# A recurrent-memory transformer on one core: order of the first steps' loads, norms, value groups and output sums

## The chip, the core and the metric

The kernel runs on one core of a Trainium2 chip, as one launch. The metric is the device time of an execution in microseconds (us). Five engines work beside each other, each through its own list of instructions in order: TensorE (PE in the profile; its weight loads are PEld), VectorE (DVE), ScalarE (ACT), GpSimd (POOL) and SyncE (SP), which here issues loads and stores. ACT and POOL can issue loads as well. An engine waits at an instruction until the semaphores that it names are reached; what stands behind it waits too.

## The reference

Two layers of the same kind are applied one after the other, with the same weights. In each, attention over segments with a memory carried from segment to segment, and then a dense layer, each behind a layer norm and with a residual:

```
x = x + A(layernorm(x));  x = x + B(layernorm(x))      # layer 0
x = x + A(layernorm(x));  x = x + B(layernorm(x))      # layer 1

A:  mem = mem0                                          # 8 x 512
    for s in range(64):                                 # segments of 32 tokens
        h = concat([mem, xs])                           # 40 x 512
        q, k, v = h Wq, h Wk, h Wv                      # 32 heads of 128
        p = softmax(mask(q k^T / sqrt(128)))            # 40 x 40 for each head
        o = (p v) Wo                                    # 40 x 512
        mem = o[:8];  output o[8:]
B:  relu(x w1) w2                                       # 512 -> 1376 -> 512
```

x is 2048 x 512, all inputs are bfloat16. The memory makes the segments a chain: a step's queries and keys need the memory that the step before has made. The values of tokens do not depend on it and can be made at any time before.

## The kernel before

**Steps.** The work is written as 68 steps. Step k handles segment k of layer 0 and segment k - 4 of layer 1, where they exist (`layers`): steps 0 to 3 have layer 0 alone ("single"), steps 4 to 63 have both, steps 64 to 67 have layer 1 alone. Step 0 is written out in `first_step`, the others in `step`. In each: queries and keys of 16 heads (`qk`, tiles `qp`, copied by ACT to QT and by DVE to KT), the scores (`sp`), a softmax (`exponentials` and `softmax`: DVE `mx`, `es`, `sm`, ACT's exponential, the product P_sb or P1_sb), the same for the other 16 heads, turns of the probabilities (`tp`, PT0, PT_sb), their product with the values (`pv`), copies of that into OTm (memory rows) and OTx (token rows), and the output of the memory rows (`output_mem`, tile `wo`).

**The end of a step.** `new_memory` copies `wo` to `wm` on ACT, turns it on PE (`mt`), and copies `mt` twice: `to_values` into HTm, from which `memory_values` makes the memory's values (`vm`, copied by ACT to VmS), and `to_queries` into HT, from which the next step's `qk` starts. Some token rows travel with the memory rows ("ride") and are picked out by `output_ride` (`xp`). `prepare` makes the statistics for the next norm.

**Fillers.** Work that is not part of this chain is put in between. `output_x` makes the token rows of the step before from OTx, in parts named by `block`: where the rows are 32, either by quarters of the 512 columns (line 405: four matmuls of 128 columns for each head) or, where `by_heads` holds, by two heads and two halves at once (line 400: two matmuls of 256 columns for each head). `add_output` then sums the pieces into the residual R on DVE: by quarters four sums of 32x128 (line 470), by heads four sums of 32x256 (line 461). `dense_h` and `dense_y` make the dense layer of the step two before; `dense_y` is cut at `f_mid`, the rest comes after `output_mem` in the steps that are not `ahead` (1 and 2).

**Values.** `values0(p, n)` makes one group of layer 0's values: 64 tokens (pair p of segments) by 1024 columns (n and n + 1), eight matmuls into a bank `vp`, a copy by ACT to a staging tile, and a write to DRAM by SP (`vd`). The matmuls of a group can be parted (`lo`, `hi`). Pairs 1, 3, 5 and 7 have four groups each. Step 0 makes eleven of the twelve groups of pairs 1, 3, 5; `values_at` puts (5,6), (7,0) and (7,2) into step 1, (7,4) into step 2's `new_memory` and (7,6) into step 4. The values are read back into Vs by `load_values`. Staging tiles are slices of w1_sb and w2_sb in step 0 (`slots`, before the dense weights are loaded there), later tiles of the tag `vst` with five buffers, shared with VmS, `wm` and the input tiles 1 to 3.

**Inputs.** Input tile n holds tokens 128n to 128n + 127. It is loaded (`load_xb`), normed (`moments_x` on DVE with a power on POOL, `normalize` on DVE), and turned (`inputs_T`: four transposes on PE and a copy by ACT for the first four tiles) into xT0. `tokens_in` copies a segment's columns to HT on POOL.

**What sets the order.** PE, DVE, SP and POOL execute in the order in which the program is written (`manual_schedule`); ACT's order, and which buffer of a tag is taken, come from the planner. SP's list begins with the loads: input tile 0, half of Wq, mem0, input tile 1, half of Wk, half of Wv, then (`load_rest`) input tile 2, the other halves, Wo in five parts, input tile 3.

## Time and profile before

| what | value |
|---|---|
| time, median of 3 runs | 1578.87 us (1577.22 to 1578.91) |
| the profiled execution: its own time, its span | 1578.9 us, 1577.0 us |
| busy: PE, PEld | 1546.3 us (98%), 1283.1 us (81%) |
| busy: DVE, ACT, POOL | 1274.7 us (81%), 736.2 us (47%), 349.1 us (22%) |
| granted TensorE clock, mean | 1.000 |
| read from and written to HBM | 65.41 MB, 45.35 MB |

The span runs from the first to the last instruction; the execution's own time is 1.9 us longer. Busy is the time in which at least one instruction of the engine ran. In the page's 40 slices of the span (39.4 us each) PE is busy 0.5 of the first, 0.8 of the second and at least 0.9 of all that follow but the last, which has 0.8; the DMA engines are busy 0.9 of the first slice, 0.7 of the second and 0.1 to 0.4 after it. Step 0's first `qp` matmul starts at 16.34 us, step 1's at 51.83, step 2's at 72.62, step 3's at 93.08, step 4's at 111.99, step 5's at 135.25. After an instruction's line in the timeline, brackets give the idle time of its engine before it and what ended that.

### The profile page before, as it was taken

The page shows a single profiled execution, that of the slowest core. Times are in us where ns is not written, and L with a number is a line of the kernel's source. Part 1 is how long each engine was busy: PE and PEld are TensorE (multiplying, and loading weights), DVE is VectorE, ACT ScalarE, POOL GpSimd, SP SyncE. Part 2 cuts the span into 40 slices and gives each one's busy share as a digit, 9 for nine tenths or more (in the row PEclk, how much of TensorE's full clock was granted, in tenths as well). Part 3 has the DMA queues.
Part 4 walks back from the last instruction along what each step waited for, and adds up shares of the span by engine and source line. Part 5 has one row for each costly group of instructions (what it writes and reads, how often), then busy time and mean ns, then how long its engine had stood idle before and what let it go on. Part 6 is the DMA issues. An engine that isn't in the chain of part 4 may idle for free. (4 is left out here: it accounts for less than half of the span.)

```text
span 1577.0 us, 95035 instructions
## 1 busy us (share of the span) xinstructions
PE 1546.3 (98%) x42802; PEld 1283.1 (81%) x42802; DVE 1274.7 (81%) x3300; ACT 736.2 (47%) x1778; POOL 349.1 (22%) x670
## 2 busy tenths in 40 slices
PE   5899999999999999999999999999999999999998
PEld 3577888888888888889888888988888898888876
DVE  3578888888888888888888888888888888888866
ACT  3435445454544545454454545445454544545443
POOL 2012212222222222222122222212222221222110
PEclk9999999999999999999999999999999999999999
DMA  9733342444444344344433433343443333334331
GB/s 370 244 81 75 87 84 81 80 95 82 73 92 84 79 82 97 81 74 91 84 80 80 99 81 75 88 84 80 77 95 81 71 88 80 82 75 95 76 69 41
DMA packets 222133, 146.26 MB, mean 93 GB/s; under 512 B 123576, under 2 KB 216096, under 8 KB 221728
## 3 DMA queue, kind: packets, MB, share of 16 engines
q1 hardware_dynamic: 218560, 135.96, 37.5%
q8 instruction: 336, 5.51, 1.5%
q0 software_dynamic: 3072, 4.20, 1.1%
q14 instruction: 69, 0.57, 0.1%
q10 hardware_dynamic: 96, 0.03, 0.0%
HBM read 65.41 MB, written 45.35 MB: 70 GB/s over the span
## 5 line engine op out<-in xcount | busy, mean ns | idle before, releaser
L601 ACT CAST QT<-qp 128x480 bf16<-128x480 f32 (+3 forms) x408 | 201.1, 493 | 432.1 <-PE qp L595 432.0
L595 PE MATMUL qp<-HT,Wq_sb 128*128 128x80 bf16 (+1 forms) x8704 | 370.0, 200 | 1.8 <-POOL HT L828 1.2
L595 PEld LDWEIGHTS <-Wq_sb 128*128 128x128 bf16 x8704 | 325.2, 100 | 33.0 <-issue 25.9
L595 PE MATMUL qp<-HT,Wk_sb 128*128 128x80 bf16 (+1 forms) x8704 | 347.3, 200 | 1.5 <-DMA Wk_sb<-in_A_Wk_dram 1.2
L595 PEld LDWEIGHTS <-Wk_sb 128*128 128x128 bf16 x8704 | 319.5, 100 | 2.6 <-DMA Wk_sb<-in_A_Wk_dram 1.7
L668 POOL TENSOR_TENSOR P_sb<-es,sm 128x320 bf16<-128x320 f32 x185 | 130.6, 719 | 712.9 <-ACT QT L601 273.7
L603 DVE CAST KT<-qp 128x480 bf16<-128x480 f32 (+3 forms) x408 | 220.2, 565 | 35.4 <-PE qp L595 32.9
L647 DVE TENSOR_REDUCE mx<-sp 128x8 f32<-128x320 f32 x256 | 114.9, 486 | 133.3 <-PE sp L629 131.6
L377 PE MATMUL wox<-Wo_sb,OTx 128*64 128x256 bf16 x2880 | 174.1, 274 | 0.1
L377 PEld LDWEIGHTS <-OTx 128*64 128x64 bf16 x2880 | 150.0, 110 | 3.7 <-issue 0.6
L653 ACT ACTIVATE es<-es 128x320 f32<-128x320 f32 x256 | 109.5, 468 | 61.5 <-DVE es L651 61.0
L839 PE MATMUL vm<-Wv_sb,HTm 128*32 128x512 bf16 x2176 | 129.4, 379 | 1.8 <-DVE KT L603 1.0
L637 PE MATMUL wo<-Wo_sb,OTm 128*32 128x512 bf16 x2144 | 128.8, 380 | 0.5
L358 PE MATMUL v<-Wv_sb,xnT 128*32 128x512 bf16 x2048 | 129.0, 378 | 0.0
L663 DVE TENSOR_REDUCE sm<-es 128x8 f32<-128x320 f32 x256 | 117.3, 458 | 12.8 <-ACT es L653 4.4
L621 DVE CAST sp<-maskb 128x320 f32<-128x320 bf16 x256 | 118.3, 483 | 0.0
L651 DVE TENSOR_TENSOR es<-sp,mx 128x320 f32<-128x320 f32 x256 | 113.5, 481 | 1.5
L547 PE MATMUL sp<-w_sb,hT 128*64 128x256 bf16 (+4 forms) x1452 | 104.0, 276 | 0.0
L843 ACT CAST VmS<-vm 128x512 bf16<-128x512 f32 x134 | 78.5, 585 | 44.5 <-PE vm L839 42.7
L526 PE MATMUL hp<-xnT,w_sb 128*128 128x64 bf16 (+1 forms) x2948 | 98.4, 192 | 0.4 <-DVE xnT L449 0.4
L222 POOL TENSOR_TENSOR mv<-mv,mhalf_t 128x1 f32<-128x1 f32 x82 | 45.6, 557 | 225.7 <-DVE mv L221 225.7
L839 PEld LDWEIGHTS <-HTm 128*32 128x32 bf16 x2176 | 54.6, 97 | 48.9 <-issue 3.2
(132 smaller groups left out, 2089.3 us busy)
## 6 DMA issues: line engine op xcount, KB each, us to landing
vd<-vst SPq DMA_DIRECT2D x181, 128.0 KB
Vs<-vd SPq DMA_DIRECT2D x90, 256.0 KB
vmd<-VmS SPq DMA_DIRECT2D x134, 128.0 KB
Vs<-vmd SPq DMA_DIRECT2D x254, 32.0 KB
Vs<-vmd SPq DMA_DIRECT2D x60, 128.0 KB
Wq_sb<-in_A_Wq_dram SPq DMA_DIRECT2D x2, 2048.0 KB
Wk_sb<-in_A_Wk_dram SPq DMA_DIRECT2D x2, 2048.0 KB
Wv_sb<-in_A_Wv_dram SPq DMA_DIRECT2D x2, 2048.0 KB
```

Source lines behind the costliest of these rows:

```text
L358: nc.tensor.matmul(vp[32 * j:32 * j + 32, :], lhsT=tokens[:, c4, :], rhs=Wv_sb[:, c4, n * 512:(n + 1) * 512], start=(c4 == 0), stop=(c4 == ...
L377: nc.tensor.matmul(out[64 * j:64 * j + nr, 0:256], lhsT=lhsT, rhs=rhs[:, 256 * j:256 * j + 256], start=start, stop=stop, tile_position=(0, ...
L595: nc.tensor.matmul(qp[:, hi, 0:ncol], lhsT=W_sb[:, c4, h * Dh:(h + 1) * Dh], rhs=HT[:, c4, a_lo:a_hi, :], start=(c4 == 0), stop=(c4 == NC4 ...
L601: nc.scalar.copy(out=dst[:, 0:nh, a_lo * L:a_hi * L], in_=qp[:, 0:nh, 0:ncol])
L603: nc.vector.tensor_copy(out=dst[:, 0:nh, a_lo * L:a_hi * L], in_=qp[:, 0:nh, 0:ncol])
L621: nc.vector.tensor_copy(out=sp_tiles[a], in_=maskb2)
L637: nc.tensor.matmul(wo[32 * j:32 * j + 32, :], lhsT=OTm[:, h, n, 2 * M * c:2 * M * c + 4 * M], rhs=Wo_sb[:, h, :], start=(h < 4), stop=(h > ...
L647: nc.vector.tensor_reduce(out=mxs[a][:], in_=sp, axis=AX.X, op=ALU.max)
L651: nc.vector.tensor_tensor(out=es[:], in0=sp, in1=mxs[a][:].unsqueeze(2).to_broadcast([128, 8, L]), op=ALU.subtract)
L663: nc.vector.tensor_reduce(out=sm[:], in_=es[:], axis=AX.X, op=ALU.add)
L668: eng.tensor_tensor(out=P, in0=es[:], in1=sm[:].unsqueeze(2).to_broadcast([128, 8, L]), op=ALU.mult)
L839: nc.tensor.matmul(vp[32 * j:32 * j + 32, :], lhsT=HTm[:, c4, :], rhs=Wv_sb[:, c4, n * 512:(n + 1) * 512], start=(c4 == 0), stop=(c4 == NC ...
```

## The change

- The loads of input tile 0, of mem0 and of input tile 1 are issued by ACT, at the head of its list; SP's list begins with Wq's half.
- At the start, tile 0 is normed and turned and its tokens are copied to HT before mem0 is turned; tile 1 follows. The zeroing of P_sb, P1_sb and OTm on POOL comes after that, with the load of the first residual between.
- Group (5,6) is made in step 0: three quarters of it in `new_memory`, the rest after `output_ride`. Its staging tile is a slot. Group (7,6) is made in the same way in step 1, group (7,4) in step 1 with (7,0) and (7,2). Steps 2 and 4 make none.
- Group (5,4)'s copy in step 0 is done by DVE.
- In step 0, `to_queries` comes before `to_values`.
- Tile 3's norm moves from within step 1's first `qk` to behind `memory_values`, its turn to within the second `qk`.
- `dense_y` of step 2 is cut at 7 instead of 9.
- `by_heads` holds for step 3 too, so that the token rows of step 3, made in step 4, are made and summed by heads.

```diff
     def load_xb(n):
...
-        nc.sync.dma_start(out=xbs[n][:], in_=A_x[0, 128 * n:128 * n + 128, :])
+        queue = nc.scalar if n < 2 else nc.sync
+        queue.dma_start(out=xbs[n][:], in_=A_x[0, 128 * n:128 * n + 128, :])
 
     load_xb(0)
+    nc.scalar.dma_start(out=mem0[0:M, :], in_=A_mem0[0, :, :])
+    load_xb(1)
...
     load_w(Wq_sb, Wq_v, 0)
-    nc.sync.dma_start(out=mem0[0:M, :], in_=A_mem0[0, :, :])
-    load_xb(1)
     load_w(Wk_sb, Wk_v, 0)
...
-    def values0(p, n, lo=0, hi=NC4, pool=None, stage=None, late=False):
+    def values0(p, n, lo=0, hi=NC4, pool=None, stage=None, late=False, by_vector=False):
...
-            nc.scalar.copy(out=vst, in_=vp[:])
+            (nc.vector.tensor_copy if by_vector else nc.scalar.copy)(out=vst, in_=vp[:])
...
     def by_heads(k):
-        return k == LAST or len(layers(k + 1)) == 1
+        return k in (DELTA - 1, LAST) or len(layers(k + 1)) == 1
...
-    def output_ride(k):
+    around = {0: (5, 6), 1: (7, 6)}
+
+    def output_ride(k, stage=None):
...
+        if k in around:
+            values0(*around[k], 3, NC4, stage=stage)
...
-        elif k < 5:
-            todo = [(0, 0, NC4)] if k == 4 and lo else []
...
-            return {1: [(5, 6), (7, 0), (7, 2)], 2: [(7, 4)], 4: [(7, 6)]}.get(k, [])
+            return {1: [(7, 0), (7, 2), (7, 4)]}.get(k, [])
...
         values1(k + 1, 0)
-        if k == 2:
-            values0(*values_at(k)[0])
+        if k in around:
+            values0(*around[k], 0, 3)
...
+        if k == 0:
+            to_queries()
         to_values()
-        to_queries()
+        if k:
+            to_queries()
...
-                    values0(p, n, stage=next(slots))
+                    values0(p, n, stage=next(slots), by_vector=(p, n) == (5, 4))
...
-            output_ride(0)
+            output_ride(0, next(slots))
...
-            if k == 1:
-                def behind():
-                    normalize(nc.vector, xbs[3], xbs[3], moments_x(3), 0, 128)
...
                 memory_values(k)
-                inputs_T(3)
+                normalize(nc.vector, xbs[3], xbs[3], moments_x(3), 0, 128)
...
             if k == 1:
+                inputs_T(3)
                 load_dense()
...
-        f_mid = 9 if ahead or k == 2 else 5
+        f_mid = 9 if ahead else 7
...
+        m = moments_x(0)
+        normalize(nc.vector, xbs[0], xbs[0], m, 0, 128)
+        inputs_T(0)
+        tokens_in(0)
         tp = transpose_pe(mem0)
...
-        for n in range(2):
-            m = moments_x(n)
-            normalize(nc.vector, xbs[n], xbs[n], m, 0, 128)
-            inputs_T(n)
+        m = moments_x(1)
+        normalize(nc.vector, xbs[1], xbs[1], m, 0, 128)
+        inputs_T(1)
+        nc.gpsimd.tensor_copy(out=HTm[:, :, 2 * M:32], in_=spare_T(0))
+        nc.gpsimd.memset(P_sb[:], 0.0)
         load_x(0)
-        nc.gpsimd.tensor_copy(out=HTm[:, :, 2 * M:32], in_=spare_T(0))
-        tokens_in(0)
+        nc.gpsimd.memset(P1_sb[:], 0.0)
+        nc.gpsimd.memset(OTm[:], 0.0)
```

More of the change, by code (lines that the diff above doesn't have):

```diff
@@ L196 @@
     P_sb = const.tile([128, 8, 128], BF)
-    nc.gpsimd.memset(P_sb[:], 0.0)
     P1_sb = const.tile([128, 16 * L + 24], BF)
-    nc.gpsimd.memset(P1_sb[:], 0.0)
     PT_sb = const.tile([128, 8, 2, L], BF)
@@ L205 @@
     OTm = const.tile([128, H, 2, 6 * M], BF)
-    nc.gpsimd.memset(OTm[:], 0.0)
     sp_banks, sp_tiles = [], []
```

## The prediction

> **What bounds the kernel now.** I read the page first, then busy time by stretches, then the timeline of the first 135 us, then PE's own waits and the completion counts of the loads.

> ```profile
> span 1577.0 us, 95035 instructions
> PE 1546.3 (98%) x42802; PEld 1283.1 (81%) x42802; DVE 1274.7 (81%) x3300; ACT 736.2 (47%) x1778; POOL 349.1 (22%) x670
> ...
> 4.00:48.00 44.00, 30.98 (x556) 18.51 (x557) 16.55 (x46) 16.25 (x36) 7.94 (x15) 1.00 1.05 388
> 48.00:133.00 85.00, 78.43 (x2326) 59.56 (x2328) 58.85 (x162) 35.47 (x93) 12.81 (x27) 1.00 0.44 123
> 133.00:1520.00 1387.00, 1386.62 (x38435) 1166.40 (x38427) 1159.88 (x2987) 663.13 (x1597) 318.78 (x601) 1.00 0.39 83
> ```

> The last three lines give length, busy time of PE, PEld, DVE, ACT, POOL, granted clock, DMA share and GB/s. From 133 us (step 5) PE has no gap: 1386.62 of 1387.00 us. Nothing after step 4 is edited, so the result is how much earlier or later step 4 ends. Up to 48 us the DMA engines are full; from 48 to 133 us PE idles 6.6 us.

> ```profile
> 16.34 0.96 PE L595 MATMUL qp<-HT,Wq_sb 128*128 128x40 bf16 x24 [1.20 <-POOL HT L828]
> ...
> 32.75 0.77 PE L595 MATMUL qp<-HT,Wk_sb 128*128 128x40 bf16 x24 [1.19 <-DMA Wk_sb<-in_A_Wk_dram]
> ...
> 37.87 1.91 PE L332 MATMUL vf<-Wv_sb,HT 128*40 128x512 bf16 x16 [0.53 <-DMA Wv_sb<-in_A_Wv_dram]
> ...
> 51.02 0.27 PE L900 MATMUL mt<-sel,wm 128*32 128x16 bf16 x16 [0.69 <-ACT wm L892]
> ...
> 51.36 0.18 ACT L911 CAST HTm<-mt 128x32 bf16<-128x32 f32 x1 [0.40 <-PE xp L492]
> ...
> 51.58 0.19 DVE L915 CAST HT<-mt 128x32 bf16<-128x32 f32 x1 [7.56 <-ACT HTm L911]
> ...
> 51.83 0.77 PE L595 MATMUL qp<-HT,Wq_sb 128*128 128x40 bf16 x24 [0.47 <-DVE HT L915]
> ...
> 56.22 1.91 PE L839 MATMUL vm<-Wv_sb,HTm 128*32 128x512 bf16 x32 [1.02 <-DVE KT L603]
> ...
> 77.53 0.20 PE L629 MATMUL sp<-KT,QT 128*40 128x40 bf16 x1 [0.69 <-issue]
> ```

> Columns are start, length, and in brackets PE's idle time and what ended it. Twice in step 0 PE waits for weights (32.75, 37.87); the other lines are waits the change reaches.

> ```profile
> 126.01 1.05 PE L310 MATMUL vp<-Wv_sb,xT 128*64 128x512 bf16 x8
> ...
> 127.05 0.63 DVE L668 TENSOR_TENSOR P_sb<-es,sm 128x320 bf16<-128x320 f32 x1
> ...
> 127.71 1.18 DVE L470 TENSOR_TENSOR R<-R,wox 32x128 f32<-32x128 f32 x4
> ...
> 128.11 0.48 PE L689 MATMUL tp<-ident,P_sb 128*64 128x80 bf16 x16
> ...
> 128.92 0.41 DVE L693 CAST PT_sb<-tp 128x240 bf16<-128x240 f32 x1
> ...
> 129.39 2.04 DVE L753 CAST OTm<-pv 128x96 bf16<-128x96 f32 x8
> ...
> 129.79 1.91 PE L637 MATMUL wo<-Wo_sb,OTm 128*32 128x512 bf16 x32
> ```

> Step 4's end: DVE goes from 127.05 to 131.43 without rest, and `wo` starts 0.15 us after the first of its eight copies.

> **The change, part by part.** The sum is against the profiled execution: span 1577.0, its own time 1578.9, which is also the median of the runs shown (1578.87).

> *First loads.* Completion counts: xb0 2.96, Wq's first half 9.25, xb1 9.61, Wk's first 14.73, Wv's first 20.25, Wq's second 27.28, Wk's second 32.70, Wv's second 37.82, last piece of Wo 49.50. SP now issues xb0, Wq, mem0, xb1 (0.82 to 2.58); then Wq goes first, 0.45 us sooner, and ACT issues the three small loads ahead of its table load (three times about 0.4, then 1.28: done near 3.4; its first copy, at 13.01 now, comes no sooner than 7). The bytes stay, and xb0's 128 KB take 0.33 us at 400 GB/s, so only ramp time can be won: from 1.75 to 3.25 us some 12 of 16 engines move. Bounds for Wv's second landing: -0.5 (the whole earlier issue) and +0.3 (one small load in the way on one engine). I take -0.2, nearest to 0.45 less 0.33.

> *Turn of tile 0 first.* xb0's statistics to tokens in HT: DVE 0.68, 0.18, 0.15, POOL 0.56, DVE 0.41, PE 0.61, ACT 0.58, POOL 0.28, with handovers about 5 us from its landing: 8.5. xb1's turn stands ahead of the first `qp` on PE, after mem0's copies: about 11.7, against 16.34. Then Wk's landing (14.5), then Wv's (20.05) hold PE: 0.95 us ahead at `vf`, waiting longer at Wk's second half, where it is lost. From 32.7 on only landings count. Cost: nothing. The memsets of P_sb, P1_sb and OTm (0.95, 0.65, 2.66 on POOL) move behind the tokens and end near 18; P_sb is first written at 23.5, OTm at 42.5; load_x(0) queued between them has no reader before step 1's end.

> *Group (5,6) around step 0's memory; memory copies exchanged; (5,4) by DVE.* A pair of these matmuls takes 0.21 us (eight: 0.86 of stream, 1.05 with the tail). Six take 0.64, under the 0.69 wait for wm's copy; two take 0.21, under the 0.47. HT's copy comes first: it ends at 51.55 instead of 51.77, `qp` starts at 51.62. -0.2; bounds -0.25 and 0 (if the last two reach past the copy). (5,4)'s copy, 0.58 on ACT, ends at 50.40 and wo's last matmul at 50.32: DVE, idle 7.56 us there, frees 0.08 at most.

> *Tile 3's norm and turn later.* Its DVE work (53.60 to 55.85) stands between the copies of KT; the second and third end at 56.4 and `vm` waits 1.02. Without it they end by 54.95, `vm` follows `qp` directly. The norm then runs from 55.0 to 57.2, POOL's part as before; DVE's next client, `mx`, needs the scores at 57.2. The four turns (0.24) only change place; they wait for nothing, the norm is done a microsecond before. -1.05; bounds -1.1 and -0.8 (if `mx` slips 0.3).

> *(7,0), (7,2), (7,4) in step 1.* Three groups for three: 0. *(7,6) around step 1's memory:* 0.64 under the 0.73 wait, 0.21 under 0.34: 0, at most +0.1.

> *What this does to step 2.* The order of buffers shows that `vm`'s second copy there must wait for the landing of (7,0)'s write, and stands on ACT behind the copies of two QT. Those end at 74.9 (times of before); then 0.58, so its bank is free at 75.5, and the last QT batch, at 75.44 now, slips 0.1; two banks instead of three cost another 0.05. SP is held by the second vmd write until 75.9, but its next load, 2.18 us now, needs 0.38 elsewhere. +0.15; bounds 0 and +1.0 (write late).

> *(7,4) out of step 2, f_mid 7.* wm's copy ends at 90.05 and mt waits for (7,4) until 90.55. With eight `y` matmuls there (four: 0.21 of stream) mt starts at 90.11: -0.45; bounds -0.5, -0.2. The four fewer before the transposes win nothing: PE waits there for P_sb (0.12).

> *(7,6) out of step 4, its outputs by heads.* PE: 16 heads take 0.89 by heads (83.50 to 84.39) and 0.90 by quarters: 0. The group's 0.86 falls out, but the transposes need P_sb at 127.68: 128.11 can become 127.74 only. Then DVE: four sums of 32x256 at 0.43 (88.53, two in 0.86) for four of 32x128 at 0.295, +0.54, on the way to PT_sb and OTm. P_sb ends 127.68, sums 129.43, PT_sb 129.87, first OTm copy 130.16, `wo` 130.25 against 129.79. +0.45; bounds +0.6 (nothing hidden) and -0.35 (sums off the path). So here the freed group is not cashed; the sums are late next.

> *The 0.69 at 77.53.* PE waits for nothing but its own instructions (a 16 KB read begun at 74.38 took 1.73 us, others 1.1, beside the loads of Vs). Those loads shift by 1.5 us: I take half of it, -0.3; bounds -0.7, +0.7.

> Sum: -0.2 - 0.2 - 1.05 + 0.15 - 0.45 + 0.45 - 0.3 = -1.6: 1577.3. All low ends give -3.4, all high ends +1.9.

> [...]

> **Rivals.** A, weights sooner: of 16 completions, Wk's second half has 14 by 30.44 and the last at 32.70, Wv's 14 by 35.96 and the last at 37.82; the late ones follow instruction reads at 21.91 and 29.36. If the new order keeps these off the last pieces, both waits go: -1.7 instead of -0.2, 1575.8 or, without the 77.53 wait, 1575.4. Against: as many instructions are read as before.

> B, late write: `vm`'s second copy in step 2 gets its buffer 2 us later than reckoned, because 2.7 MB of w1 and w2 go ahead of (7,0)'s write; ACT stands, PE with it: +2, 1579.3. The DMA engines empty at 71.7 now, 3 us before the point where it counts.

> C, the slower side, instruction reads: 128 rows fewer on PE shift every later 256-row read by half. If one read in each group of four steps then meets the loads of Vs as at 77.53, that is 0.24 to 0.69 sixteen times, 4 to 11 us: 1581.5 and up. It decides from 0.3 us in each group. Against: reads fall every 4 us on all parts of a step already, and PE idles 0.38 us from 133 to 1520.

> [...]

> **Numbers.** Forecast 0.57 (its own range 1576.0 to 1578.9), A 0.2, B 0.08, C 0.1, D 0.05. 0.2% is 3.2 us, about what a measurement tells here: faster means under 1575.7. That takes most of A and a little of the forecast: 0.2; slower is C, 0.1; the rest 0.7. The range takes in A and B and leaves C out: 1575.0 to 1580.0.

> **What would show it.** First `qp` near 11.7, `vf` of the second half within 0.5 of 37.87; `vm` of step 1 near 54.7 without a wait for KT; mt in steps 0 and 1 right behind six `vp`; on ACT in step 2 a VmS copy behind two QT; in step 4 about 1 us of PE idle before `tp`, and four sums of 1.72 us before PT_sb. Wrong if Wv's landing moves by over 0.5 us, or if `wo` of step 4 starts no later after the scores than now (123.46 to 129.79, 6.33 us).

## The result and the profile after

The changed kernel is slower: 1582.12 us, median of 12 runs (1579.02 to 1584.55), beside 1577.90 us for the kernel before in 12 runs of the same chip; ratio 1.0026, 95% interval 1.0018 to 1.0034. The forecast, 1577.3 us (1575.0 to 1580.0), is missed on the slow side. The profiled execution of the changed kernel took 1582.36 us, its span is 1580.6 us.

The page of the changed kernel, and then the same three stretches (length, busy time of PE, PEld, DVE, ACT, POOL, granted clock, DMA share, GB/s):

```profile
span 1580.6 us, 94909 instructions
...
PE 1551.2 (98%) x42737; PEld 1285.6 (81%) x42738; DVE 1277.9 (81%) x3301; ACT 737.8 (47%) x1777; POOL 350.0 (22%) x670
...
q1 hardware_dynamic: 218256, 135.69, 40.3%
```

```profile
4.00:48.00 44.00, 33.15 (x564) 19.58 (x564) 16.30 (x46) 16.32 (x36) 8.19 (x13) 1.00 1.05 389
48.00:133.00 85.00, 79.20 (x2248) 59.05 (x2248) 59.89 (x161) 34.63 (x90) 12.85 (x27) 0.98 0.49 122
133.00:1520.00 1387.00, 1384.74 (x38308) 1164.68 (x38292) 1159.02 (x2981) 663.96 (x1593) 319.19 (x599) 1.00 0.42 83
```

Two things stand in the last two lines that the prediction has no term for. From 48 to 133 us the clock is 0.98. And from 133 us on, where no instruction was edited, the DMA engines are busy 42% of the time instead of 39%, at the same 83 GB/s, and TensorE idles 2.26 us instead of 0.38.

To see where the time goes, I take one instruction of every step, ACT's copy of `wo` to `wm`, and subtract its start in the kernel before from that in the changed one (us; negative is sooner):

| step | 0 | 1 | 2 | 3 | 4 | 5 | 16 | 32 | 48 | 62 | 66 |
|---|---|---|---|---|---|---|---|---|---|---|---|
| changed less before | -0.61 | -1.71 | -1.16 | -1.61 | +0.46 | +0.40 | +0.33 | +1.80 | +2.41 | +3.85 | +3.04 |

So there are three parts: steps 0 to 3 gain 1.61 us; step 4 alone loses 2.07; steps 5 to 62, which are the same instructions in the same order, lose 3.39, little by little. The steps behind 62 give 0.81 back.

The first part is what was foretold. TensorE in the timeline of the changed kernel (start, length, idle time before it and what ended that):

```profile
11.97 1.01 PE L597 MATMUL qp<-HT,Wq_sb 128*128 128x40 bf16 x24
...
31.92 0.77 PE L597 MATMUL qp<-HT,Wk_sb 128*128 128x40 bf16 x24 [0.78 <-DMA Wk_sb<-in_A_Wk_dram]
...
37.02 1.91 PE L330 MATMUL vf<-Wv_sb,HT 128*40 128x512 bf16 x16 [0.51 <-DMA Wv_sb<-in_A_Wv_dram]
```

```profile
50.41 0.27 PE L900 MATMUL mt<-sel,wm 128*32 128x16 bf16 x16
50.53 0.23 PE L492 MATMUL xp<-wm,sel 128*32 128x128 bf16 x4
50.68 0.41 PE L308 MATMUL vp<-Wv_sb,xT 128*64 128x512 bf16 x2
51.02 0.77 PE L597 MATMUL qp<-HT,Wq_sb 128*128 128x40 bf16 x24
...
54.67 1.91 PE L841 MATMUL vm<-Wv_sb,HTm 128*32 128x512 bf16 x32 [0.28 <-DVE KT L605]
```

The first `qp` starts at 11.97 instead of 16.34, the waits for `wm` and HT around 50.4 are gone, and of the wait for KT 0.28 of 1.02 us is left.

The second part, step 4's end in the changed kernel:

```profile
126.10 1.76 DVE L459 TENSOR_TENSOR R<-R,wox 32x256 f32<-32x256 f32 x4
...
126.21 0.48 PE L691 MATMUL tp<-ident,P_sb 128*64 128x80 bf16 x16 [1.02 <-POOL HT L830]
...
127.89 0.41 DVE L695 CAST PT_sb<-tp 128x240 bf16<-128x240 f32 x1
...
128.35 0.38 PE L736 MATMUL pv<-PT_sb,Vs 40*128 40x40 bf16 x15 [0.61 <-DVE PT_sb L695]
...
128.66 3.50 PE L639 MATMUL wo<-Wo_sb,OTm 128*32 128x512 bf16 x32
```

The waits are the foretold ones, and so are the four sums (1.76 us). But `wo` takes 3.50 us where it took 1.91: the granted clock is at half (0.50) from 128.51 to 131.92. Not every execution has this fall: in 4 of the 12 the recorded mean clock is 1.000, which leaves no room for 3.41 us at half (0.999 at most). These four took 1579.02, 1581.41, 1582.24 and 1582.64 us, so without the fall, too, the kernel is mostly slower than before.

The third part has one visible form. An example from step 10 of the changed kernel:

```profile
256.05 1.03 PE L597 MATMUL qp<-HT,Wq_sb 128*128 128x80 bf16 x24
257.42 1.03 PE L597 MATMUL qp<-HT,Wk_sb 128*128 128x80 bf16 x24 [0.33 <-issue]
```

The profile shows nothing that TensorE waits for in these 0.33 us (`issue`). In such time I take it to wait for its instructions, and call it so below. The packets of the trace show what else goes on: a read of instructions (16 KB, 0.92 us) begins at 254.75, and 23 packets of the kernel's own queue (8 of 4 B, 6 of 256 B, 9 of 1024 B) begun between 255.28 and 255.54 took 1.59 to 1.89 us each and end together near 257.15, where the median of such packets is 9 to 46 ns. Six such gaps over 0.1 us and one for a late `xnT` (0.53) make up 1.84 us. All of TensorE's idle time in these steps is 2.13 us, against 0.26 in the kernel before, so idle time accounts for 1.87 of the 3.39 us; the rest stands in no gap, and where it arises stays open. TensorE's own waits between 155 and 1470 us in the changed kernel (line, releaser, us, times, longest) are these two; the kernel before has no such line there:

```profile
PE qp L597 <- issue: 1.2, 5, 0.3
PE hp L528 <- DMA xnT<-XN: 0.5, 1, 0.5
```

### The profile page after: what moved, and what is told of

It reads as the page before. It is cut to its first block, busy times and chain, and to the rows that moved or that the text cites. A ratio compares the mean times of both kernels' runs of the same rounds, so it can differ in the third digit from the quotient of the medians.

```text
span 1580.6 us, 94909 instructions
## 1 busy us (share of the span) xinstructions
PE 1551.2 (98%) x42737; PEld 1285.6 (81%) x42738; DVE 1277.9 (81%) x3301; ACT 737.8 (47%) x1777; POOL 350.0 (22%) x670
## 4 chain that ended last, share of the span: by engine, by line
PE 94%; SPq 2%; DVE 1%; DMA 1%; issue 1%; ACT 0%; POOL 0%; POOLq 0%
PE qp L597 38%; PE wox L375 10%; PE wo L639 8%; PE vm L841 7%; PE v L356 7%; PE hp L528 5%; PE sp L549 5%; PE sp L631 4%; PE pv L736 3%; PE vp L308 3%; SPq L149 2%; PE tp L691 1%; SPq L137 1%; PE wox L398 1%; DMA Wo_sb<-in_A_Wo_dram 1%
## 5 line engine op out<-in xcount | busy, mean ns | idle before, releaser
L603 ACT CAST QT<-qp 128x480 bf16<-128x480 f32 (+3 forms) x408 | 201.7, 494 | 432.3 <-PE qp L597 424.8
```

The source lines that it names most:

```text
L603: nc.scalar.copy(out=dst[:, 0:nh, a_lo * L:a_hi * L], in_=qp[:, 0:nh, 0:ncol])
```

## The experiments

The theory for the third part is rival C of the prediction. A row is one instruction of TensorE, a weight load, a matmul or a semaphore instruction; in 56 steps the trace has 280 reads of 16 KB for 71655 rows, so 256 rows a read and five reads a step. Counted in the trace, three steps of a group of four have some 1299 rows and the fourth 1220: 5115 to 5117 for four steps (some 5131 in the last two groups), and 20 reads are 5120. So by this count a read falls on nearly the same five places of every step, and a shift stays. Step 4's outputs by heads take 128 rows fewer, half a read. Behind the copies to `wm` of steps 5 to 8 the reads begin near 2.8, 8.8, 12.7, 16.7 and 21.6 us after the copy in the kernel before, near 1.2, 6.3, 10.5, 14.7 and 20.1 in the changed one. Counted from the same copy, SP issues the loads of Vs between about 4.6 and 10.7 us, the transpose of XN into `xnT` between 6.2 and 8.2, and the transpose of P_sb into PT near 14.

Packets of 256 B that took 400 ns or more between 140 and 1520 us: 218 before, 1231 after. They are packets of these two transposes, and not of the loads of Vs that the prediction and the expectations name. From 167.5 to 175 us of the kernel before, the transpose of P_sb is all that SP issues, and its queue moves nothing but small packets:

```profile
DMA packets 1105, 0.34 MB, mean 46 GB/s; under 512 B 1072, under 2 KB 1072, under 8 KB 1104
...
q1 hardware_dynamic: 1056, 0.26, 16.1%
...
PT<-P_sb SPq DMA_TRANSPOSE x1
```

The transposes also hold SP for longer. In step 6, first of the kernel before, where the next read begins at 163.19 us, then of the changed kernel, where it begins at 161.60:

```profile
160.67 1.19 SPq L291 DMA_TRANSPOSE xnT<-XN  x1
```

```profile
161.07 2.72 SPq L289 DMA_TRANSPOSE xnT<-XN  x1
```

The table gives all runs. "Rows" is how many rows of TensorE stand ahead of step 5 compared with the kernel before; "step 4" and "steps 5 to 62" are what these lose against the profile of the kernel before; "long" is the count just named. The last columns are the median, and the ratio to the kernel before on the same chip with its interval. The three groups of runs had different chips, on which the kernel before took 1578.12, 1578.61 and 1578.65 us (medians), so ratios are what is compared between groups. "Step 4" and "steps 5 to 62" are read from one execution of each kernel; with 0 rows the latter spreads from -0.32 to +0.70, which says how exactly one profile tells it.

| kernel | rows | step 4 | steps 5 to 62 | long | median us | ratio |
|---|---|---|---|---|---|---|
| changed | -128 | +2.07 | +3.39 | 1231 | 1582.12 | 1.0026 (1.0018 to 1.0034) |
| changed, 128 rows more | 0 | +2.01 | -0.32 | 190 | 1579.38 | 1.0005 (0.9997 to 1.0014) |
| changed, 256 rows more | +128 | +2.02 | +3.05 | 1262 | 1583.60 | 1.0029 (1.0020 to 1.0038) |
| changed, by quarters | 0 | -0.13 | +0.22 | 166 | 1577.30 | 0.9989 (0.9981 to 0.9998) |
| before, 128 rows more | +128 | +0.25 | +3.42 | 1324 | 1584.60 | 1.0035 (1.0023 to 1.0047) |
| changed, TensorE kept busy | -106 | +0.46 | +5.28 | 1296 | 1582.36 | 1.0023 (1.0013 to 1.0032) |
| by quarters, (7,6) in step 4 | 0 | +1.56 | +0.70 | 239 | 1577.83 | 0.9996 (0.9987 to 1.0005) |
| by quarters, loads on SP | 0 | +0.06 | +0.12 | 268 | 1577.44 | 0.9993 (0.9984 to 1.0002) |
| by quarters, tile 3 early | 0 | +0.07 | +0.08 | 214 | 1579.28 | 1.0003 (0.9994 to 1.0011) |
| before, by heads | -128 | +0.46 | +3.58 | 1296 | 1583.78 | 1.0027 (1.0017 to 1.0037) |
| by quarters, 64 rows more | +64 | +1.32 | +2.51 | 310 | 1582.41 | 1.0026 (1.0017 to 1.0035) |
| changed, 64 rows more | -64 | +1.87 | +2.72 | 734 | 1579.84 | 1.0007 (0.9998 to 1.0016) |

Of the 116 transposes of XN and P_sb in steps 5 to 62, those that held SP for over 1.5 us are 4 to 9 in the kernels with 0 rows and in the kernel before, 14 with 64 rows more by quarters, and 38 to 64 in the others.

**Do the reads' places make the loss? 128 rows more.**

```diff
+    def spin(n):
+        for i in range(n):
+            nc.tensor.matmul(sp_banks[1][:, 504:505], lhsT=ident[:], rhs=maskb[:, 0:1],
+                             start=True, stop=True)
...
         tp = transpose_pe(mem0)
+        spin(64)
```

> The changed kernel with 64 pairs of a weight load and a one-column matmul on TensorE behind the turn of the memory, where TensorE waits 2.67 us for input tile 1: 128 rows, so that TensorE has 85606 rows as before the change, and its reads of 256 rows (16 KB) fall on the same places of a step as before. The theory (rival C: four steps have 5117 rows, 20 reads, so a shift of half a read made in step 4 stays in every step; reads then meet the loads of Vs) expects that the packets of 256 B over 400 ns in 140 to 1520 us fall from 1231 to some 220, that the 2.6 us lost over steps 5 to 62 go, and 1579.5 us. The rival, another cause in the transfers (first loads on ScalarE's queue, the places of the staging buffers), expects no change: 1582.1, within 0.7, and over 1000 such packets.

Measured 1579.38 us and 190 long packets; steps 5 to 62 lose nothing (-0.32). The 64 pairs do no work at all and take the ratio from 1.0026 to 1.0005. Step 4 still loses 2.01, and the start is 1.6 us later than in the changed kernel (in this profile TensorE stands 2.50 us ahead of `vf` and 1.83 us at 38.47 for its instructions), so this kernel does not get below the one before.

**Is it the place, or the pairs? 256 rows more.** The same with 40, 50 and 38 pairs at three places ahead of step 0.

```diff
+        spin(40)
         inputs_T(0)
         tokens_in(0)
+        spin(50)
         tp = transpose_pe(mem0)
+        spin(38)
```

> The changed kernel with 128 such pairs (256 rows, one whole read: 40 ahead of the turn of input tile 0, 50 ahead of the memory's, 38 behind it). The theory expects the reads where the changed kernel has them: over 1000 packets of 256 B above 400 ns, and 1582.1 us within 0.7. If the pairs help by themselves (a TensorE at work earlier, so another clock at the start), it goes with the run of 128 rows, below 1580.5.

1583.60 us, 1262 long packets, 3.05 us lost over steps 5 to 62: one whole read more, and all is as in the changed kernel. The pairs do not help by themselves.

**The same shift without the change: 128 rows more in the kernel before.** 64 pairs ahead of `tp = transpose_pe(mem0)`.

```diff
+        spin(64)
         tp = transpose_pe(mem0)
```

> The kernel before with 64 such pairs ahead of the turn of the memory, where TensorE waits for its load: 85734 rows, so the reads are shifted by half a read without any part of the change. The theory expects over 1000 packets of 256 B above 400 ns in 140 to 1520 us, instead of 218, and 2.6 us more than before, 1580.5. The rival (the transfers are slower through a part of the change) expects 1577.9 within 0.7 and some 220 such packets.

1324 long packets and 3.42 us lost over steps 5 to 62, with nothing of the change in it: the theory holds. The total, 1584.60, is above the 1580.5 expected because the start suffers: the first `qp` comes 0.37 us later, TensorE stands 1.81 us at 23.77 and 1.27 us at 40.86 for instructions, the clock is at half from 24.77 to 28.18, and step 0 ends 3.43 us late. That part belongs to the experiment and not to the theory.

How the DMA engines' load shows the shift, by the queue on which SP issues its loads, stores and transposes, from 155 to 1470 us (packets, MB, share of 16 engines). The kernel before:

```profile
q1 hardware_dynamic: 181352, 100.33, 35.7%
```

The changed kernel, and below it the kernel before with 128 rows more:

```profile
q1 hardware_dynamic: 181152, 100.16, 39.0%
```

```profile
q1 hardware_dynamic: 181374, 100.35, 40.2%
```

Nearly the same bytes occupy the engines for 3.3 to 4.5 points longer. This share is no measure of the loss either: with 0 rows it is 34.6 to 35.8%, but with 64 rows fewer it is 34.6% as well, in a profile that loses 2.72 us over steps 5 to 62.

**Step 4 by quarters, as before the change.**

```diff
     def by_heads(k):
-        return k in (DELTA - 1, LAST) or len(layers(k + 1)) == 1
+        return k == LAST or len(layers(k + 1)) == 1
```

> The changed kernel with step 4's outputs by quarters, as before the change; group (7, 6) stays in step 1. That takes back step 4's 64 pairs of 32x256 for 64 pairs more, so that TensorE has 85606 rows again. The theory expects the 2.6 us of steps 5 to 62 back through the reads; for step 4, where 2.07 us went and the clock was at half for 3.41 us: if the sums by heads are the cause of its waits, the fall of the clock goes too and the time is 1577.5; if (7, 6), which no longer fills TensorE's wait for P_sb, is the cause, the clock still falls and the time is 1579.5. If the reads have no part in it, the time is 1580 or more.

1577.30 us; ratio 0.9989 (0.9981 to 0.9998): faster than both kernels, though hardly more than can be measured. Both losses are gone at once, the reads' by the 128 rows that come back, step 4's because `wo` is no longer slow. Step 4's end in this kernel:

```profile
125.67 1.18 DVE L468 TENSOR_TENSOR R<-R,wox 32x128 f32<-32x128 f32 x4
...
125.79 0.48 PE L691 MATMUL tp<-ident,P_sb 128*64 128x80 bf16 x16 [1.00 <-POOL HT L830]
...
127.63 1.91 PE L639 MATMUL wo<-Wo_sb,OTm 128*32 128x512 bf16 x32
```

TensorE waits 1.00 us for P_sb as in the changed kernel, but the second wait, of 0.61 us for PT_sb, is not there (the sums take 1.18 us), and the clock stays.

**What is the sums' share in step 4, and what the clock's? TensorE kept busy.** 11 matmuls in the first wait.

```diff
+    def spin(n, cols):
+        for i in range(n):
+            nc.tensor.matmul(sp_banks[1][:, 320:320 + cols], lhsT=ident[:], rhs=Wo_sb[:, 0, 0:cols],
+                             start=True, stop=True)
...
             else:
+                if k == DELTA:
+                    spin(11, 192)
                 transpose_p(1, 5)
```

These matmuls write into the scores' bank, beside the scores. This kernel's output is off by a relative 0.10; I take it that step 4's scores are altered, which is not shown. The work and its order are the same.

> The changed kernel, outputs of step 4 by heads, with 11 do-nothing matmuls of 192 columns (22 rows) in the 0.99 us in which TensorE waits for P_sb in step 4. If the half clock of 128.51 to 131.92 us follows from the idle 0.99 and 0.61 us ahead of it, it goes, step 4 loses about 0.4 us against the kernel before instead of 2.07, and the time is 1580.4 us, with the loss of steps 5 to 62 left at some 3 us. If the clock falls there for another reason, or the waits are the loss, step 4 still loses 1.5 or more: 1582.

```profile
124.34 1.08 PE L975 MATMUL sp<-Wo_sb,ident 128*128 128x192 bf16 x11
...
125.43 0.48 PE L691 MATMUL tp<-ident,P_sb 128*64 128x80 bf16 x16
...
127.57 0.35 PE L736 MATMUL pv<-PT_sb,Vs 40*128 40x40 bf16 x15 [0.61 <-DVE PT_sb L695]
...
127.86 1.91 PE L639 MATMUL wo<-Wo_sb,OTm 128*32 128x512 bf16 x32
```

In step 4 it does what was expected: the clock does not fall, `wo` takes 1.91 us, and the step loses 0.46 instead of 2.07. So by heads costs 0.46 us by the later sums and 1.61 us by the clock. But the total, expected at 1580.4, is 1582.36: steps 5 to 62 lose 5.28 us instead of 3.39. That second half of the expectation ("some 3 us left") was wrong. The 22 rows that I added make the reads begin 0.1 to 0.3 us earlier in a step, and the transpose of P_sb holds SP for over 1.5 us 35 times instead of 20; that these rows cost the 1.89 us more is likely by the theory and was not tested.

**One part alone: by heads in the kernel before.**

```diff
     def by_heads(k):
-        return k == LAST or len(layers(k + 1)) == 1
+        return k in (DELTA - 1, LAST) or len(layers(k + 1)) == 1
```

> The kernel before with one part of the change alone: step 4's outputs by heads. That makes TensorE's rows 85478 and shifts the reads by half a read; group (7, 6) is still in step 4. The theory expects a loss of some 3.4 us over steps 5 to 62 with over 1000 packets of 256 B above 400 ns, and in step 4 itself 0.5 to 2 us, by whether the clock falls there: 1581.5 to 1583.5 us. If heads are only a matter of step 4, 1578.5 to 1580.

1583.78 us, 1296 long packets, 3.58 us lost over steps 5 to 62. With (7,6) still in step 4 to fill the wait, the clock stays, and step 4 loses the same 0.46 us. This one line of the change by itself makes the loss. From 133 to 1520 us TensorE stands 0.75, 0.41, 0.49, 0.27, 0.25, 0.23 and 0.24 us for instructions, and for nothing else over 0.2.

**How wide are the good places? 64 rows on either side.** 32 pairs in step 4's wait for P_sb, once by quarters and once by heads, written to the bank that the transposes then overwrite.

```diff
-    def transpose_p(hf, cut=4):
+    def transpose_p(hf, cut=4, pairs=0):
...
             tp = ps_c.tile([128, ns, 2, L], F32, tag="c", name="tp")
+            for _ in range(pairs if s0 == 0 else 0):
+                nc.tensor.matmul(tp[:, 0, 0, 0:1], lhsT=ident[:], rhs=maskb[:, 0:1], start=True, stop=True)
...
-                transpose_p(1, 5)
+                transpose_p(1, 5, 32 if k == DELTA else 0)
```

> The changed kernel with step 4's outputs by quarters and 32 do-nothing pairs (64 rows, a quarter of a read) in TensorE's wait of 0.96 us for P_sb in step 4, so that the start is as in the run by quarters and only the later reads stand 64 rows earlier. How far the good places reach is not known: if a quarter of a read is still good, 1577.3 us and under 300 packets of 256 B above 400 ns; if it meets the loads of Vs, 1579 to 1582 and over 600.

> The changed kernel, outputs by heads, with the same 32 pairs in the same wait: 64 rows fewer than the kernel before instead of 128, the quarter of a read on the other side. In step 4 the pairs fill the wait, so by the run with 11 matmuls there the clock stays and step 4 loses 0.4 to 0.7 us. If the good places reach to 64 rows fewer, 1578.5 us; if they do not, 1580.5 to 1583.

64 rows more are bad, 64 fewer are not settled. 64 rows more: 1582.41 us, 2.51 us lost over steps 5 to 62, and a stand of 1.71 us for instructions in step 4 itself. It has only 310 long packets, so their number is a sign of the bad half and not the measure of the loss; what the loss at this place consists of stays open. It is there without a fall of the clock: the five executions with a mean clock of 1.000 have a median of 1581.51 us. 64 rows fewer: 2.72 us in the profile, which is of an execution near the top of its runs (1576.51 to 1582.88, median 1579.84) and has a fall of the clock. In six of these 11 executions the mean clock is 1.000, and their median is 1578.20 us; that of the other five is 1582.34. So where the clock does not fall, the time is that of a good place (1578.5 was expected for it). Why the others are 4.1 us slower, when a fall in step 4 costs 1.6, stays open. The second expectation on this kernel was also wrong: the clock fell in step 4, though the pairs filled the wait.

```profile
125.19 0.95 PE L688 MATMUL tp<-maskb,ident 128*128 128x1 bf16 x32
126.28 0.48 PE L693 MATMUL tp<-ident,P_sb 128*64 128x80 bf16 x16
...
128.70 3.34 PE L639 MATMUL wo<-Wo_sb,OTm 128*32 128x512 bf16 x32
```

**Terms of the first steps.** Three parts undone one by one in the kernel by quarters, which keeps the reads where they are good.

Input tile 3 as before:

```diff
+            if k == 1:
+                def behind():
+                    normalize(nc.vector, xbs[3], xbs[3], moments_x(3), 0, 128)
...
-                normalize(nc.vector, xbs[3], xbs[3], moments_x(3), 0, 128)
+                inputs_T(3)
...
-                inputs_T(3)
                 load_dense()
```

> The changed kernel with step 4's outputs by quarters and the norm and turn of input tile 3 where the kernel before has them in step 1. The prediction's term for it is 1.05 us, so 1578.35 us, with TensorE's wait for KT ahead of the memory's values of step 1 (1.0 us in the kernel before, 0.26 in the changed one) back. If the gain of step 1 is that of (7, 6) or of the loads, no change: 1577.3 within 0.3.

Ratio 1.0003 against 0.9989, so about 2.2 us, twice the price expected, with both intervals some 0.0017 wide. The wait is there (this kernel's timeline; by quarters there is none), and step 1 loses 1.26 us, most of it in this wait; step 2 loses another 0.55:

```profile
55.83 1.91 PE L841 MATMUL vm<-Wv_sb,HTm 128*32 128x512 bf16 x32 [1.01 <-DVE KT L605]
```

In step 2 TensorE stands 0.67, 0.37, 0.54 and 0.41 us for instructions instead of 0.37 and 0.54.

The first loads on SP as before:

```diff
-        queue = nc.scalar if n < 2 else nc.sync
-        queue.dma_start(out=xbs[n][:], in_=A_x[0, 128 * n:128 * n + 128, :])
+        nc.sync.dma_start(out=xbs[n][:], in_=A_x[0, 128 * n:128 * n + 128, :])
...
-    nc.scalar.dma_start(out=mem0[0:M, :], in_=A_mem0[0, :, :])
-    load_xb(1)
...
     load_w(Wq_sb, Wq_v, 0)
+    nc.sync.dma_start(out=mem0[0:M, :], in_=A_mem0[0, :, :])
+    load_xb(1)
```

> The changed kernel with step 4's outputs by quarters and the first three loads on SyncE's queue in the order of the kernel before. By the prediction's term the loads on ScalarE's queue are worth 0.2 us, by the trace of the changed kernel, whose step 0 ends 0.61 us sooner, up to 0.6: 1577.5 to 1577.9 us. If ScalarE's queue had any part in the slower transfers of steps 5 to 62, the time would be below 1577.3.

Ratio 0.9993 (0.9984 to 1.0002) against 0.9989: worth 0.6 us, which the two intervals do not tell from none. In its profile step 0 ends 1.75 us later than by quarters, of which 1.1 is left at step 4; but there the clock is at half from 20.87 to 27.70 us, so this is not the price of the loads alone. ScalarE's queue has no part in steps 5 to 62: by quarters these loads are on it and 0.22 us is lost there, 0.12 without them, while the kernel before by heads loses 3.58 with the loads on SP.

Group (7,6) back in step 4:

```diff
-    around = {0: (5, 6), 1: (7, 6)}
+    around = {0: (5, 6)}
...
-            return {1: [(7, 0), (7, 2), (7, 4)]}.get(k, [])
+            return {1: [(7, 0), (7, 2), (7, 4)], 4: [(7, 6)]}.get(k, [])
...
+        elif k < 5:
+            todo = [(0, 0, NC4)] if k == 4 and lo else []
```

> The changed kernel with step 4's outputs by quarters and group (7, 6) back in step 4, where it was before the change. The theory says that (7, 6) is worth as much in step 1 as in step 4: in step 4 it covers the 0.96 us for which TensorE waits for P_sb, in step 1 the wait for wm (0.73 us in the kernel before) comes back: 1577.3 us, as the run by quarters, within 0.4. A rival: the wait in step 1 is covered by what else is there, and the time is 1576.4.

1577.83 us; ratio 0.9996 (0.9987 to 1.0005), not told apart from the run by quarters. In step 1 the two profiles take the same time (both gain 1.45 us): the waits for `wm` and HT are back (0.74 and 0.34 us), as expected, and the group's own time is gone. In step 4 this one stands 1.59 us for instructions; it is of an execution of 1579.15 us, the third slowest of 11, so I draw nothing from that stand.

## Why the prediction was wrong

*Steps 0 to 3: right in sum, not in every piece.* The terms up to step 4 add up to -2.05 us; the changed kernel gained 1.61, the one by quarters 2.03. That the second fits so well is partly luck, since misses cancel. The loads and group (5,6): -0.4 foretold, -0.81 at step 1's first `qp` (51.83 to 51.02), of which -0.61 is there already at the copy to `wm` ahead of it. Tile 3 later: -1.05 foretold, -0.90 from that `qp` to step 1's copy to `wm`, and -1.26 by undoing it. (7,4) out of step 2: -0.45 foretold, and the mark behind it moves by -0.45. Wv's second landing moved by 0.84 us (37.82 to 36.98), more than the 0.5 allowed. The staging write of (7,0) held nothing up for long: the second VmS copy stands behind two QT copies at 73.91, as foretold. The stall of 0.69 us at 77.53, of which half was to go, became two of 0.58 and 0.54: step 2 lost 0.55 instead of gaining 0.15. (The high ends of the prediction's terms add up to +1.7 and not to +1.9, which changes nothing.)

*Step 4: mechanism right, one term missing.* "+0.45" for the later sums is what two kernels without the clock's fall lost (0.46 and 0.46), and `wo` started 0.47 us later after the scores than before (121.86 to 128.66, against 6.33 us). Missing was the clock: 1.61 us in the profiled execution, where TensorE was idle for 1.63 of the 3.41 us before the fall (1.02 and 0.61 us in the two waits above). The kernel before did not show it: its granted clock is 1.00 from 19.85 to 1576.32 us. The prediction gave a fall a chance of 0.05 (D), an estimate, and at one place only, in the wait before Wk's second half. In the changed kernel that wait is 0.78 us, and the clock fell in step 4; in the profile of the kernel by quarters it fell where D had it, at 31.86, behind a wait of 2.06 us, and step 0 still ended 0.49 us sooner than before: the wait for Wv absorbed nearly all of it.

*Steps 5 to 67: the step that failed is the sentence "Nothing after step 4 is edited, so the result is how much earlier or later step 4 ends."* It is wrong by 3.4 us. What decided is rival C, which was given a chance of 0.1. It had the right mechanism, a shift by half a read that stays, and at its low end the right price: 0.24 us in each group of four steps, where 3.39 us in 14.5 groups are 0.23. What the reads were to meet, the loads of Vs, is half of it: the waits that can be listed do come beside them (in step 10 SP issues them from 254.25 to 257.54 us, and TensorE waits until 257.42), but the packets of 256 B that are delayed are those of the transposes. And its total, 1581.5 us and up, was reached only with the 1.6 us of the clock, which it did not have: that is luck. The argument held against it, "reads fall every 4 us on all parts of a step already", fails on a count that the trace of before would have given: 5115 to 5117 rows in four steps against 5120 in 20 reads. The reads fall on five places and not on all, and the kernel before had them in good ones. That TensorE idled only 0.38 us there was no reason for safety: it shows that the reads did no harm where they were, and that there was no slack to take up a late one.

What is not settled: why 64 rows more cost nearly as much as 128 with so few long packets, where the 1.5 us arise that stand in no gap, and how a read of 0.92 us (step 10) leaves TensorE without instructions 1.4 us after its end. The runs show that the places of the reads decide. That they do so by meeting the transposes and the loads of Vs is argued from the packets: a kernel in which these are moved and the reads left was not tried.

## What to carry to other kernels

Here TensorE has no slack over a long periodic stretch (0.38 us idle in 1387), and a shift of its instruction reads by 64 or 128 rows ahead of that stretch cost 2.5 to 3.6 us in it in the profiles. So count the rows of a period; where, as here, they are close to a whole number of reads (5115 to 5117 rows against 5120), compare an edit ahead with the same rows put back as do-nothing pairs in a wait before judging it. And read a new wait on TensorE together with its neighbours: here 1.0 and 0.6 us close together cost 1.6 us more through the clock, while either alone (1.00 us by quarters, 0.61 us with TensorE kept busy) came without a fall in step 4.
